# Attention and gated feed-forward on one core: block 0 divided by its sums behind the value products, two maxima taken from PSUM, one group's turn by DVE and DMA, and a new order

## The chip, the cores and the metric

The kernel runs on 1 core of one Trainium2 chip. The metric is the device time of one execution in microseconds; the median of the runs shown is given, and beside it the profiled execution.

## The reference

Inputs are q, k and v of 4 batches, 8 heads, 768 positions and 64 dimensions in float32, and two weight matrices, w_in (512 x 2048) and w_out (2048 x 512).

```
k_sum = k.reshape(B, H, 24, 32, D).max(axis=3)      # one summary key per 32 keys
v_sum = v.reshape(B, H, 24, 32, D).mean(axis=3)
scores = [q.k / 8 where |i - j| < 16 else -1e9,  q.k_sum / 8 + log(32)]
a = exp(scores - max);  a = a / (sum(a) + 1e-9)
x = a @ [v, v_sum]                                   # 3072 tokens x 512
h = x @ w_in;  out = (h * cos(h)) @ w_out
```

## The kernel before

**Blocks and groups.** The 3072 tokens are eight blocks of 384, two to a batch. A block's attention is done in four groups, one for each pair of heads, named a, b, c and d; a0 is pair a of block 0, c1 pair c of block 1. A group has six tiles of 64 queries, and each tile sees 96 neighbouring keys and 24 summary keys, so its scores are 128 x 720 (128 partitions: two halves of 64 queries; 6 times 120 columns).

**One group's path (class Group).** `load_q`, `load_k`, `load_v` (three DMAs) and `load_vs` (two) bring the data. In blocks 0 and 1, PE turns q and k (`turn_q`, `turn_k`) and ACT or DVE copy them out; two products with an identity lay the masks in two PSUM banks (`place_masks`), and `scores` adds the products, one bank for each head. `scale` copies each bank to SBUF (two copies), `maximum` is a DVE reduction over the 720 columns (L588), `less_max` subtracts it on POOL (L593), `exp` runs on ACT (L606), `sums` adds up on DVE (L609, over 121 columns a row, the last a constant 1e-9), `inverse` is a reciprocal on DVE (L614), and `normalize` multiplies on POOL (L617). Then the probabilities are turned: in groups that are not "moved" PE does six transposes (`turn_p`, L626) and ACT or DVE two copies (`place_p`, tile pt); in "moved" groups DVE transposes 32 x 32 squares (`square_p`, L640), one DMA writes them to memory (`move_out`) and four read them back in place (`move_in`). `values` (L670) multiplies v by pt, 12 products, and its output already has the dimensions on the partitions, as the feed-forward needs it. `x_high` rounds it to the matmul format, `x_low` is the rest (DVE, L356, tile xl).

**Feed-forward (class Step).** Step s of a block and a slice f of 128 hidden columns: `up` is 12 products (L714), then ACT and DVE compute the gate (`turns`, `residue`, `sine`, `square`, `gate`), the result is split in a high and a low part, and `down` and `down_low` are nine products (L770). Six steps of block 0 (s0 to s5) come first, then the 16 of block 1, then the other ten of block 0, then the other blocks.

**Weights (class Slice).** A slice f of w_in and w_out, w0 to w15, is loaded by two DMAs of 512 KB and split into a high and a low part of 1024 columns: `magnitude` on ACT (L388), `clamp` (L393), `shift` (L399), `last_bits` (L407) and `first_bits` (L415) on DVE, `high_part` (a cast, ACT or DVE), `low_part` (a subtraction on POOL or DVE). Step s0 needs w0, and so on.

**Order.** The whole order is written out by hand in the string `ORDER`. A token is owner, method and arguments: `a0.tp.0.3` is `turn_p` of the first four tiles of a0 into bank 3, `w5.fb.1` is `first_bits` of slice 5 into stage buffer 1. The loop at the end calls the method of each token in turn, and each engine, and SP for the DMAs, keeps its instructions in that order; waits between engines are put in by the framework.

The short names: q, k, v, m are the loads; tq, tk turns; cq, ck copies; ks key summaries; ms masks; sc scores; z copies of the scores; mx maximum; su less_max; ex exp; sm sums; iv inverse; nm normalize; tp, cp turn and copy of the probabilities; pt, po, pi squares, move out, move in; va values; xh, xl high and low part of x; for slices l, ab, cl, sh, lb, fb, hi, lo in the order of the list above; for steps up, tu, re, si, sq, ga, hi, lo, dh, dl, and ta, tb, st, sb for the results.

## Time and profile before

| | |
|---|---|
| runs shown, median (3 runs) | 663.17 us (660.64 to 663.44) |
| profiled execution | 661.89 us |
| its span, first to last instruction | 660.1 us |
| PE busy | 632.6 us (96%) |
| DVE / ACT / POOL busy | 449.7 / 363.9 / 221.8 us |
| mean granted TensorE clock | 0.987 |

In a row of the timeline the columns are start (us from the span's start), duration, engine, line, operation, output<-input, shapes and count; in brackets stands how long the engine was idle before it and what it waited for. A row of the stretches gives the stretch, its length, and for each engine the busy time and the number of instructions, then the granted clock (1 is 2.4 GHz, 0.5 is 1.2 GHz), the share of the DMA engines and the rate. A row of the chain is start, duration and what held the end of the program at that time. "late", "x" and "sc" are tiles: late buffers hold raw weights and, early on, data of the groups.

### The profile page before, as it was taken

To read this page: it belongs to the slowest core of one execution; us is meant where nothing else is said; L and a number is where in the kernel's file an instruction comes from. 1 tells how busy PE (TensorE), PEld (TensorE's weight loads), DVE (VectorE), ACT (ScalarE), POOL (GpSimd) and SP (SyncE) were. 2 spreads that over 40 slices of the span, in tenths; PEclk is the share of its full clock that TensorE was granted. 3 is DMA by queue.
4 is the path that set the end of the run, shared out by engine and by line. 5 is a ranking of instruction groups with operands and counts; after the bars stand their busy time and mean duration, and the time that the engine had idled before them with its cause. 6 is when DMAs were issued, how large, how long until landed. Compare 5 with 4: busy or idle time off the path is not lost.

```text
span 660.1 us, 13282 instructions
## 1 busy us (share of the span) xinstructions
PE 632.6 (96%) x5141; PEld 560.2 (85%) x5141; DVE 449.7 (68%) x798; ACT 363.9 (55%) x640; POOL 221.8 (34%) x219
## 2 busy tenths in 40 slices
PE   6478999999999999999999999999999999999996
PEld 5256889989988998898898899889889989899985
DVE  4887999887855576668797777576876756433344
ACT  2656977776554485437477464356554645444342
POOL 4784896764430342301323411112330212010110
PEclk9869999999999999999999999999999999999999
DMA  9997906544243244525445433424364332000001
GB/s 224 259 271 203 276 15 223 169 109 71 55 122 85 91 124 132 127 59 114 111 107 135 147 98 97 114 43 85 115 163 104 92 94 70 5 1 17 16 17 48
DMA packets 167158, 72.68 MB, mean 110 GB/s; under 512 B 136824, under 2 KB 155832, under 8 KB 167096
## 3 DMA queue, kind: packets, MB, share of 16 engines
q1 hardware_dynamic: 167096, 71.84, 40.9%
q8 instruction: 40, 0.66, 0.4%
q14 instruction: 22, 0.18, 0.1%
HBM read 53.72 MB, written 15.73 MB: 105 GB/s over the span
## 4 chain that ended last, share of the span: by engine, by line
PE 86%; DMA 5%; SPq 3%; POOL 2%; DVE 1%; issue 1%; ACT 1%; DVEq 0%; POOLq 0%; ACTq 0%
PE banks L770 39%; PE banks L714 39%; PE banks L569 4%; PE banks L670 3%; DMA late<-in_moe_w_out_dram 3%; DMA late<-in_v_dram 1%; SPq L456 1%; POOL w L356 1%; DMA late<-in_q_dram 1%; POOL gl L356 1%; SPq L493 1%; POOL stage L393 0%; ACT stage L388 0%; PE banks L556 0%; DVE m L588 0%
## 5 line engine op out<-in xcount | busy, mean ns | idle before, releaser
L714 PE MATMUL banks<-xh,w 128*128 128x384 f32 x1024 | 272.1, 337 | 0.1
L770 PE MATMUL banks<-w,gh 128*128 128x512 f32 x768 | 198.1, 393 | 0.2 <-ACT gh L350 0.2
L714 PEld LDWEIGHTS banks<-xh,w 128*128 128x128 f32 x1024 | 185.9, 188 | 2.8 <-ACT pt L350 0.4
L714 PE MATMUL banks<-xl,w 128*128 128x384 f32 x512 | 171.4, 335 | 0.0
L770 PEld LDWEIGHTS banks<-w,gh 128*128 128x128 f32 x768 | 142.6, 188 | 29.0 <-ACT gh L350 0.5
L724 ACT ACTIVATE t<-banks 128x384 int32<-128x384 f32 x128 | 62.5, 489 | 133.6 <-DVE gl L356 54.9
L356 POOL TENSOR_TENSOR gl<-t,gh 128x384 fp32r<-128x384 f32 x55 | 56.6, 1029 | 221.4 <-ACT gh L350 86.0
L770 PE MATMUL banks<-w,gl 128*128 128x512 f32 x384 | 109.8, 394 | 0.1
L727 DVE SCALAR_TENSOR_TENSOR t<-t,banks 128x384 f32<-128x384 int32 x128 | 70.0, 548 | 56.9 <-ACT t L724 56.2
L732 ACT ACTIVATE t<-t 128x384 f32<-128x384 f32 x128 | 66.7, 523 | 66.3 <-DVE t L727 66.0
L714 PEld LDWEIGHTS banks<-xl,w 128*128 128x128 f32 x512 | 96.1, 188 | 1.6
L739 DVE SCALAR_TENSOR_TENSOR t<-t,banks 128x384 f32<-128x384 f32 x128 | 69.3, 546 | 41.2 <-ACT t L735 41.0
L770 PEld LDWEIGHTS banks<-w,gl 128*128 128x128 f32 x384 | 71.1, 188 | 14.6 <-DVE gl L356 0.2
L593 POOL TENSOR_TENSOR sc<-sc,m 128x720 f32<-128x720 f32 x28 | 40.1, 1431 | 129.2 <-DVE m L588 129.2
L735 ACT ACTIVATE t<-t 128x384 f32<-128x384 f32 x128 | 65.8, 521 | 2.1
L617 POOL TENSOR_TENSOR sc<-sc,r 128x720 f32<-128x720 f32 x28 | 39.5, 1411 | 51.4 <-DVE r L614 50.3
L350 ACT CAST gh<-t 128x384 fp32r<-128x384 f32 x68 | 34.7, 510 | 33.2 <-PE banks L770 16.5
L356 DVE TENSOR_TENSOR gl<-t,gh 128x384 fp32r<-128x384 f32 x73 | 41.7, 572 | 12.6 <-ACT gh L350 6.5
L356 POOL TENSOR_TENSOR w<-stage,w 128x1024 fp32r<-128x1024 f32 x15 | 36.2, 2416 | 10.0 <-ACT w L350 8.6
L352 DVE CAST gh<-t 128x384 fp32r<-128x384 f32 x60 | 23.2, 386 | 22.2 <-PE banks L770 20.4
L580 DVE SCALAR_TENSOR_TENSOR sc<-banks,mask 128x360 f32<-128x360 f32 x48 | 24.4, 524 | 19.2 <-PE banks L569 19.0
L569 PEld LDWEIGHTS banks<-kd,qd 64*64 64x64 f32 x1344 | 28.4, 135 | 9.4 <-issue 6.7
(102 smaller groups left out, 620.7 us busy)
## 6 DMA issues: line engine op xcount, KB each, us to landing
pd<-stage SPq DMA_DIRECT2D x22, 384.0 KB
late<-in_moe_w_in_dram SPq DMA_DIRECT2D x16, 512.0 KB
late<-in_moe_w_out_dram SPq DMA_DIRECT2D x16, 512.0 KB
pt<-pd SPq DMA_DIRECT2D x66, 96.0 KB
vn<-in_v_dram SPq DMA_DIRECT2D x52, 120.0 KB
out_dram<-stage SPq DMA_DIRECT2D x23, 256.0 KB
kn<-in_v_dram SPq DMA_DIRECT2D x24, 192.0 KB
qn<-in_q_dram SPq DMA_DIRECT2D x92, 48.0 KB
```

The costliest lines, as they stand in the source:

```text
L350: eng.copy(out=out, in_=in_)
L356: eng.tensor_tensor(out=lo, in0=src, in1=hi.bitcast(F32), op=ALU.subtract)
L569: nc.tensor.matmul(out=self.sp[hh][s * QT : (s + 1) * QT, c, lo : lo + n], lhsT=self.qd[rows, t * QT : (t + 1) * QT], rhs=self.kd[rows, ke ...
L593: nc.gpsimd.tensor_tensor(out=self.sc, in0=self.sc, in1=self.m.unsqueeze(2).broadcast_to([P, U, NK]), op=ALU.subtract)
L617: nc.gpsimd.tensor_tensor(out=self.sc, in0=self.sc, in1=self.r.unsqueeze(2).broadcast_to([P, U, NK]), op=ALU.mult)
L714: nc.tensor.matmul(out=self.h, lhsT=w_of(name, self.f)[:, c * P : (c + 1) * P], rhs=x_of(self.blk, part, c), start=n == 0, stop=n == last,)
L724: nc.scalar.activation(out=self.t.bitcast(I32), in_=self.h, func=AF.Copy, scale=1.0 / TWO_PI)
L727: nc.vector.scalar_tensor_tensor(out=self.t, in0=self.t.bitcast(I32), scalar=-TWO_PI, in1=self.h, op0=ALU.mult, op1=ALU.add)
L732: nc.scalar.activation(out=self.t, in_=self.t, func=AF.Sin, scale=0.5)
L735: nc.scalar.activation(out=self.t, in_=self.t, func=AF.Square, scale=math.sqrt(2.0))
L739: nc.vector.scalar_tensor_tensor(out=self.t, in0=self.t, scalar=-1.0, in1=self.h, op0=ALU.add, op1=ALU.mult)
L770: nc.tensor.matmul(out=self.acc[i], lhsT=g[:, i * P : (i + 1) * P], rhs=w_of(name, self.f), start=self.first and n == 0, stop=self.last an ...
```

## The change

Four things:

- `LATE`: in block 0's four groups `sums` and `normalize` go. The probabilities are turned undivided, with the constant column of 1e-9 as a row 121. `values` takes pt as the stationary side and v as the moving one, so its output has the queries on the partitions, and after each of the 12 products a second one with a column of ones gives the sum of its row. `inverse` then reads these sums from PSUM, the new `divide` (xn) multiplies on DVE from PSUM into one SBUF tile shared by the four groups, and the new `turn_x` (tx) turns the result with three transposes on PE; `x_high` and `x_low` follow as before.
- `PMAX`: in a1 and c1, `maximum` reads the scores in PSUM, from two banks side by side, instead of the copy in SBUF.
- `TURNS`: b2 becomes a "moved" group (its six transposes and two copies go).
- A new `ORDER`: 2245 tokens for 2246.

```diff
+PMAX = "00001010000000000000000000000000"
+LATE = "11110000000000000000000000000000"
-TURNS = ("00000000011111111111111111111111", "00000000001111111111111111111111")
+TURNS = ("00000000011111111111111111111111", "00000000011111111111111111111111")
...
+            self.late = LATE[blk * NG + pr : blk * NG + pr + 1] == "1"
+            self.rows = NK + 1 if self.late else NK
+            self.pmax = int(PMAX[blk * NG + pr : blk * NG + pr + 1] or "0")
...
         def maximum(self):
             m = self.m = att.tile([P, U], F32, name="m", bufs=2)
+            if self.pmax:
+                i = self.first_bank
+                nc.vector.tensor_reduce(
+                    out=m.rearrange("p (c h) -> p h c", h=2),
+                    in_=banks[:, i : i + 2, : QC * NK].rearrange("p h (c n) -> p h c n", n=NK),
+                    axis=AX.X, op=ALU.max,
+                )
...
+                return
...
         def inverse(self):
-            if self.fused:
+            if self.late:
+                self.r = att.tile([P, U], F32, name="r", bufs=2)
+                nc.vector.reciprocal(out=self.r, in_=self.xw[:, :, D])
+                return
...
-                nc.tensor.transpose(out=pT[:, t - lo, :], in_=self.sc[:, t, :], identity=ident)
+                nc.tensor.transpose(out=pT[:, t - lo, :], in_=self.all[:, t, : self.rows], identity=ident)
...
         def values(self, i):
+            if self.late:
+                self.xw = bank(i)[:, : U * (D + 1)].rearrange("p (u n) -> p u n", u=U)
+                for t in range(U):
+                    c, s = divmod(t, 2)
+                    for hh in range(2):
+                        p, to = self.pt[2 * c + hh][s], self.xw[s * QT : (s + 1) * QT, 2 * c + hh]
+                        nc.tensor.matmul(
+                            out=to[:, :D], lhsT=p[:NK], rhs=self.vn[:, t, hh * D : (hh + 1) * D],
+                            start=True, stop=True,
+                        )
+                        nc.tensor.matmul(out=to[:, D:], lhsT=p, rhs=ones[: self.rows], start=True, stop=True)
+                return
...
+        def divide(self):
+            nc.vector.tensor_tensor(
+                out=self.xq.rearrange("p (u n) -> p u n", u=U), in0=self.xw[:, :, :D],
+                in1=self.r.unsqueeze(2).broadcast_to([P, U, D]), op=ALU.mult,
+            )
+
+        def turn_x(self, i):
+            self.xps = bank(i)[:, :TB]
+            for c in range(QC):
+                cols = slice(c * P, (c + 1) * P)
+                nc.tensor.transpose(out=self.xps[:, cols], in_=self.xq[:, cols], identity=ident)
...
+    Group.xq = carve(x1[3], 0, P, TB)
```

The new order, by queue, where it matters early. SP before and after (loads):

```
before  ... d0.q w0.l c0.v c0.m w2.l a0.v a0.m d0.m w5.l c1.m b1.q w3.l d1.m c1.q a1.q d0.v w4.l a1.m a1.v b0.m b1.m d1.q b0.v c1.v v1_0.l w8.l
after   ... d0.q w0.l d0.m a0.v w2.l c0.m a0.m w5.l c1.m b1.q c0.v a1.q w3.l d0.v b0.m w4.l c1.q b1.m b0.v a1.v c1.v a1.m d1.q v1_0.l w8.l
```

DVE from v0_0's halving to b0.xl, before and after:

```
before  v0_0.h a0.iv v0_1.s c0.mx w1.cl w1.sh w1.lb w1.fb d0.mx w0.cl c0.sm w0.sh c0.iv w0.lb w2.cl w0.fb d0.sm w2.sh d0.iv w2.lb w2.fb w5.cl a0.xl w5.sh b0.mx w5.lb w5.fb b0.sm c0.xl b0.iv w3.sh a1.mx w3.lb d0.xl w4.cl w4.sh c1.mx w4.lb a1.sm b0.xl
after   v0_1.h v0_0.h v0_1.s c0.mx w1.cl w1.sh w1.lb w1.fb w0.cl d0.mx w0.sh w0.lb w0.fb w2.cl w2.sh b0.mx w2.lb a0.iv w2.fb a0.xn w5.cl c0.iv w5.sh c0.xn w5.lb a0.xl w3.cl w5.fb w3.sh d0.iv c0.xl d0.xn a1.mx w4.cl w3.lb w4.sh c1.mx a1.sm b0.iv d0.xl a1.iv b0.xn w4.lb b0.xl
```

ACT around the same time, before and after:

```
before  w1.ab b0.z.1 b0.z.0 d0.cq d0.ck.1 c0.ex d0.z.1 d0.z.0 w0.ab w1.hi w2.ab a0.cp.0 d0.ex a0.cp.1 w0.hi w5.ab a0.xh c0.cp.0 c0.cp.1 w2.hi
after   w1.ab d0.cq a0.cp.0 b0.z.0 a0.cp.1 d0.z.1 w0.ab d0.z.0 w1.hi w2.ab c0.ex w0.hi b0.z.1 w5.ab d0.ex c0.cp.0 c0.cp.1 w2.hi b1.cq a0.xh
```

PE from a0's value products to s1.up, after:

```
a0.va c0.tp.0 b1.tq c0.tp.1 c0.va a0.tx d0.tp a1.tq a1.ms c0.tx a1.sc d0.va b0.tp.0 c1.tq c1.ms d0.tx b0.tp.1 c1.sc b0.va b1.ms b1.sc b0.tx d1.tq a1.tp.0 s0.up d1.ms a1.tp.1 d1.sc s1.up
```

a1's tokens are `a1.z.1 ... a1.z.0 a1.mx` and c1's `c1.z.1 ... c1.mx c1.z.0`. On PE, between b2.pt and b2.va stand s19.dl, s20.dh, s20.dl, c2.sc, a2.va, s21.dh, s21.dl, s24.up, s25.up and d2.sc. On ACT d1.ex and b1.ex now stand one behind the other. v0_1's halving and the clamp of w3 move from POOL to DVE. The end is now `s127.tb.2.a s127.ta.1.0.v s127.ta.0.1.a s127.sb.2 s127.ta.2.v s127.st.1 s127.st.0 s127.st.2`, where before ACT took the first half of chunk 2 and DVE all the rest.

## Rows read from the trace of the kernel before

**Rows 1.** The page, part 1: busy time, share of the span, instructions.
```profile
PE 632.6 (96%) x5141; PEld 560.2 (85%) x5141; DVE 449.7 (68%) x798; ACT 363.9 (55%) x640; POOL 221.8 (34%) x219
```

**Rows 2.** Busy time by stretch: PE, PEld, DVE, ACT, POOL, clock, DMA share, GB/s.
```profile
21.73:58.88 37.15, 23.28 (x343) 17.02 (x344) 32.32 (x40) 24.11 (x41) 27.04 (x18) 0.77 0.80 216
26.00:42.00 16.00, 7.67 (x69) 6.19 (x69) 15.64 (x20) 9.88 (x15) 11.28 (x7) 0.57 0.92 258
58.88:70.00 11.12, 10.29 (x120) 8.51 (x119) 9.58 (x13) 9.00 (x17) 6.31 (x5) 1.00 1.03 325
70.00:93.00 23.00, 22.73 (x175) 19.46 (x174) 21.46 (x34) 21.03 (x35) 21.56 (x18) 1.00 0.49 137
93.00:655.00 562.00, 562.00 (x4320) 504.98 (x4320) 373.50 (x691) 302.91 (x538) 156.30 (x143) 1.00 0.35 92
```

**Rows 3.** Timeline of PE: a0.va, b1.tq, c0.va, b0.va, start of s0.up.
```profile
32.58 1.65 PE L670 MATMUL banks<-pt,vn 120*64 120x64 f32 x24 [5.44 <-ACT pt L350]
...
37.75 0.88 PE L502 MATMUL banks<-ident,late 128*128 128x128 f32 x3 [2.35 <-DMA late<-in_q_dram]
...
39.26 1.55 PE L670 MATMUL banks<-pt,x 120*64 120x64 f32 x24 [0.21 <-ACT pt L350]
...
56.71 0.92 PE L670 MATMUL banks<-pt,vn 120*64 120x64 f32 x24 [2.27 <-DMA vn<-in_v_dram]
...
58.88 0.43 PE L714 MATMUL banks<-xh,w 128*128 128x384 f32 x1
```

**Rows 4.** Timeline of DVE: v0_0.h, c0.mx, w1.cl, w2.sh, d0.iv, b0.xl, tail copy.
```profile
18.38 1.22 DVE L259 TENSOR_TENSOR late<-late 96x1024 f32<-96x1024 f32 x1 [1.36 <-DMA late<-in_v_dram]
...
21.73 0.89 DVE L588 TENSOR_REDUCE m<-late 128x6 f32<-128x720 f32 x1
22.93 0.70 DVE L393 TENSOR_SCALAR stage<-stage 128x1024 f32<-128x1024 f32 x1 [0.31 <-ACT stage L388]
...
34.87 1.21 DVE L399 TENSOR_SCALAR banks<-stage 128x1024 int32<-128x1024 int32 x1
36.00 0.17 DVE L614 RECIPROCAL r<-r 128x6 f32<-128x6 f32 x1
...
58.18 0.56 DVE L356 TENSOR_TENSOR xl<-banks,xh 128x384 fp32r<-128x384 f32 x1 [1.14 <-ACT xh L350]
...
655.57 0.42 DVE L808 TENSOR_SCALAR last<-banks 128x256 f32<-128x256 f32 x1 [0.63 <-ACT last L806]
```

**Rows 5.** Chain that ended last, early pieces: start, duration, what.
```profile
18.30 7.46 DMA late<-in_moe_w_out_dram
...
25.78 0.33 SPq L477
...
31.82 5.28 DMA late<-in_moe_w_out_dram
```

**Rows 6.** Groups by line and shape, 100 to 655 us: sums, normalize, square_p.
```profile
L617 POOL TENSOR_TENSOR sc<-sc,r 128x720 f32<-128x720 f32 x24 | 33.9, 1414 | 51.4 <-DVE r L614 50.3 <-ACT sc L606 1.0
...
L609 DVE TENSOR_REDUCE r<-sc 128x6 f32<-128x726 f32 x24 | 21.6, 898 | 6.4 <-ACT sc L606 6.2
...
L640 DVE STREAM_TRANSPOSE stage<-sc 128x768 f32<-128x768 f32 x22 | 21.3, 970 | 8.0 <-POOL sc L617 7.9
```

**Rows 7.** Chain that ended last, later pieces: scores, value products, six transposes.
```profile
165.37 1.02 PE banks L569 x36
166.38 0.85 PE banks L670 x24
...
174.34 0.66 PE banks L626 x6
```

**Rows 8.** Timeline of SP's queue: c0.v's first two issues, b1.q.
```profile
19.20 1.99 SPq L477 DMA_DIRECT2D x<-in_v_dram  x2
...
34.11 1.03 SPq L456 DMA_DIRECT2D late<-in_q_dram  x2
```

**Rows 9.** Timeline of ACT: a copy of c1's scores.
```profile
52.58 0.45 ACT L350 COPY late<-banks 128x360 f32<-128x360 f32 x1
```

More of the change, by code (lines that the diff above doesn't have):

```diff
@@ L173 @@
-s123.hi.a s124.si s123.lo.p s124.sq s124.ga s126.up.3 s124.hi.v s124.lo.v s127.up.4 s126.tu s125.tu s125.re s126.re
-s123.dh s126.si s125.si s123.dl s125.sq s126.sq s124.dh s125.ga s125.hi.v s125.lo.v s124.dl s127.tu s125.dh s127.re
-s126.ga s127.si s126.hi.v s127.sq s125.dl s126.lo.v s126.dh s127.ga s127.hi.a s126.dl s127.lo.p s127.dh s127.dl
-s127.ta.2.a s127.ta.0.0.v s127.st.2 s127.tb.2.v s127.st.0 s127.ta.1.1.v s127.sb.2 s127.st.1
+b0.k a0.q a0.k c0.k d0.k b0.tk.0.0 c0.q b0.tk.1.1 a0.tq.2 v0_1.l a0.tk.0.3 a0.tk.1.4 a0.ck.0.a a0.ks.0 v0_0.l
@@ new lines @@
+a0.ms.5.6 a0.ck.1.a a0.ks.1 a0.cq.v c0.tk.0.7 b0.ck.0.v a0.sc b0.q b0.ks.1 c0.ck.0.v c0.tk.1.3 a0.z.1.a b0.ks.0 w1.l
+a0.z.0.v c0.tq.4 a0.mx d0.tk.0.2 c0.cq.a d0.tk.1.6 d0.q c0.ms.0.5 c0.ck.1.a a0.su d0.ks.1 d0.ks.0 c0.ks.0 a0.ex w0.l
+c0.ks.1 v0_1.h.v c0.sc v0_0.h.v c0.z.0.a b0.tq.4 d0.ck.0.a b0.ms.7.3 b0.cq.a v0_1.s.v v0_0.s.p d0.ck.1.a a0.tp.0.0
+c0.z.1.a b0.ck.1.a b0.sc w1.ab.0 c0.mx d0.m d0.tq.2 w1.cl.v c0.su d0.ms.6.1 a0.v d0.cq.a w1.sh.4.5 a0.cp.0.a a0.tp.1.2
+b0.z.0.a d0.sc w2.l a0.cp.1.a w1.lb d0.z.1.a c0.m w0.ab.0 w1.fb.1 a0.m d0.z.0.a w0.cl.v w1.hi.a d0.mx w5.l w1.lo.p
@@ L177 @@
+s123.dl s125.sq s126.re s125.ga s126.si s124.dh s125.hi.a s126.sq s125.lo.p s124.dl s126.ga s125.dh s127.tu s126.hi.a
+s127.re s126.lo.v s127.si s125.dl s127.sq s126.dh s127.ga s127.hi.v s126.dl s127.lo.p s127.dh s127.dl s127.tb.2.a
+s127.ta.1.0.v s127.ta.0.1.a s127.sb.2 s127.ta.2.v s127.st.1 s127.st.0 s127.st.2
 """
@@ L307, in tile_kernel @@
     qd0 = const.tile([P, TB], F32, name="qd")
+    ones = const.tile([P, 1], F32, name="ones")
+    nc.vector.memset(ones, 1.0)
     kmax = const.tile([P, NB // 2, BLOCK // 2], F32, name="kmax")
@@ L551, in score_banks @@
             self.sp = [bank(i)[:, : QC * NK].rearrange("p (c n) -> p c n", c=QC) for i in two]
+            self.first_bank = two[0]
         def place_masks(self, *two):
@@ L597, in exp @@
         def exp(self):
-            self.r = att.tile([P, U], F32, name="r", bufs=2)
-            if self.fused:
+            if not self.late:
+                self.r = att.tile([P, U], F32, name="r", bufs=2)
+            if self.pmax == 2:
+                for u in range(U):
+                    c, h = divmod(u, 2)
+                    nc.scalar.activation(
+                        out=self.sc[:, u, :], in_=self.sp[h][:, c, :], func=AF.Exp, bias=self.m[:, u : u + 1],
+                        accum_out=self.r[:, u : u + 1],
+                    )
+            elif self.fused:
                 for u in range(U):
@@ L623, in turn_p @@
             lo, hi = ((0, 4), (4, U))[j]
-            pT = self.pT[j] = bank(i)[:NK, : (hi - lo) * P].rearrange("p (t n) -> p t n", t=hi - lo)
+            pT = self.pT[j] = bank(i)[: self.rows, : (hi - lo) * P].rearrange("p (t n) -> p t n", t=hi - lo)
             for t in range(lo, hi):
-                nc.tensor.transpose(out=pT[:, t - lo, :], in_=self.sc[:, t, :], identity=ident)
+                nc.tensor.transpose(out=pT[:, t - lo, :], in_=self.all[:, t, : self.rows], identity=ident)
         def place_p(self, j, eng):
@@ L631, in place_p @@
                 self.pts = att.tile([P, U * P], F32, name="pt")
-            pt = self.pts[:NK].rearrange("p (t n) -> p t n", t=U)
+            pt = self.pts[: self.rows].rearrange("p (t n) -> p t n", t=U)
             copy(eng, pt[:, lo:hi, :], self.pT[j])
@@ L846, in tile_kernel @@
     n_v, n_k, n_s = U * P, KC * P, U * NKP
-    x1 = [xp.tile([P, 2 * TB], F32, name=f"x1_{i}", tag=t) for i, t in enumerate(("xh01", "xl01", "xh11"))]
+    x1 = [xp.tile([P, 2 * TB], F32, name=f"x1_{i}", tag=t) for i, t in enumerate(("xh01", "xl01", "xh11", "xl11"))]
     qd1 = carve(late[2], 2 * n_k, P, TB)
@@ L907, in tile_kernel @@
             su="less_max", ex="exp", sm="sums", iv="inverse", nm="normalize", tp="turn_p", cp="place_p",
-            va="values", xh="x_high", xl="x_low",
+            va="values", xn="divide", tx="turn_x", xh="x_high", xl="x_low",
         ),
```

291 lines of the change are left out of this document (145 added, 146 removed).

## The prediction

> **What bounds the kernel now.** The page's first part comes first: PE is busy for 632.6 of 660.1 us [rows 1], so 27.5 us are all the idle time that a new order could give back, and everything else is PE's own work. The table of stretches says where that idle time lies: from 93 to 655 us there is none, from 70 to 93 us 0.27 us, from 58.88 to 70 us 0.83 us [rows 2]; the rest, 26.4 us, lies before 58.88 us and in the last 5 us. PE's timeline gives the moments and what it waited for: a0's value products begin at 32.58 us after 5.44 us for ACT's copy of the turned probabilities (pt), b1's q at 37.75 after 2.35 us for its load, c0's value products at 39.26, b0's at 56.71 after 2.27 us for v, and the first up-projection, s0.up, at 58.88 [rows 3]. From there PE has work in its queue nearly without a gap. So the time of the kernel is **the start of s0.up, plus PE's work behind it, plus what PE idles behind it**, and I price the change in these three.
>
> What sets the start of s0.up is DVE. Between 21.73 and 58.88 us it is busy for 32.32 of 37.15 us, and from 26 to 42 us for 15.64 of 16 [rows 2]; its last low part (b0.xl) starts at 58.18 and runs 0.56 us, and s0.up follows [rows 3, 4]. Its second string is SP's queue: in the chain the issue at 25.78 follows the landing at 25.76 of a transfer issued at 18.30, eight issues earlier, so SP can be held by what has not landed [rows 5].
>
> **Block 0 divided late.** Out go, for each of four groups, the sum over the probabilities (0.90 us on DVE) and the scaling by POOL (1.41) [rows 6]; three of the four sums lie behind 21.73 us, which frees 2.7 us of DVE. In come a division of 128x384 out of PSUM, which I take as the low part of the same shape and source, 0.56 [rows 4]: 2.2 us of DVE. The reciprocal stays (0.17 each), but reads what PE has made. POOL's 5.6 us are worth nothing by themselves: POOL is not the bound before 58.88 us, and from 70 us the four scalings are long done.
>
> PE gets twelve more products a group with one moving column, and three transposes. The twelve are 24 records. Bounds from rows: the 48 records of the scores, of which the chain lists 36, take 1.02 us (0.021 each), the 24 of the values 0.85 (0.035) [rows 7]; 0.5 to 0.85 us, and I take 0.7. A transpose is 0.11 (six in 0.66) [rows 7]. That is 1.0 us a group, 4 us in all, up to twice that while the granted clock is at half (mean 0.57 from 26 to 42 us [rows 2], between the levels of 1.2 and 2.4 GHz). All of it stands ahead of s0.up in PE's queue, where PE has some 21 us of idle time to cover it, so as PE work it costs nothing; only the piece on c0's path counts, and it is in the walk below. The Trainium skill, "TensorE: Matmul & The Clock Gate", section "Wait — 56ns, not 53.3ns?", states that the spacing of small matmuls never falls below about 25 ns, and that about 62 ns each bind where the decode is not done in hardware; by the latter the 24 records would cost, as an estimate from that page, 1.5 us a group, s0.up would come about 0.8 us later, and the sum would be -1.9 instead of -2.7 us. The 0.021 us of the scores' records speak against it, and I keep 0.7.
>
> **A new kind of wait.** Before, the reciprocal followed DVE's own sum. Now a0.iv, c0.iv, d0.iv and b0.iv wait for PE's value products, which wait for ACT's copies and for v; behind each stand the bit passes of the weights, the division and the low parts, and for those wait w5's, w3's and w4's casts and s0.up. I follow DVE's new queue from the latest of the early ones. c0.v is issued behind b1.q rather than at 19.20 us [rows 8]. SP loses some 2.5 us to the wait for v's sums (d0.m now follows the weights directly) and saves as much by c0.v's absence, so b1.q keeps its place, its issue ending near 35.1 us; PE used it 2.6 us after that end [rows 3, 8]. So c0.v is issued until about 37 us and lands near 39.5. c0's value products then begin at 39.5, against 39.26 before, and last 1.55 [rows 3] plus some 0.8 for the new ones at half clock: c0.iv at 41.9. **From there to b0.xl DVE's queue holds** seven passes over a slice (1.21 each), two clamps (0.70), seven divisions or low parts (0.56), three reductions over 720 (0.89) and three reciprocals (0.17), 17.0 us; neighbours overlap by about 0.08 (34.87 + 1.21 against 36.00) [rows 4], so 22 of them take 15.3. That gives 57.2; for b0's round trip through PE and ACT I add 0.2. **s0.up at 57.4, or -1.5 us.** The bounds are from DVE never waiting (54.3, the first rival) to waits like the two longest above (64, the second).
>
> **The maximum taken in PSUM** (a1, c1): worth 0. The idea would save a copy of 0.45 us [rows 9] ahead of each maximum. But DVE's copy at 655.57 waited 0.63 us for ACT, which read the other half of the same bank [rows 4]: reads of one bank by two engines are put in a row. In the new order both copies of a1 stand ahead of a1.mx, which therefore waits for both as before; c1.mx goes ahead of one copy, and that copy then waits for c1.mx, with the subtraction behind it. The bounds are -0.9 (both copies hidden) and +0.9 us (ACT held by c1.z.0 for a reduction), on engines that are not PE; I keep 0.
>
> **b2's probabilities by DVE and DMA.** Six transposes go from PE in the stretch where it never idles: 0.66 us [rows 7]. DVE's transposition costs 0.97 [rows 6] against a copy of 512 columns that goes, and ACT loses a copy of 256: both have room (373.5 and 302.9 of 562 us [rows 2]). SP gets five issues more behind b2.nm. From square to value products the new order leaves PE two up-projections, two and a half down steps, two scores and a value product, some 12 us, which cover a write and a read back; if that cover fell short PE would wait up to 5 us (as the longest pt wait [rows 3]), and I give that no part of the forecast. Gain **-0.66**.
>
> **The rest of the order.** a1's first four transposes move ahead of s0.up: **-0.44** at 0.11 each. v0_1's halving and w3's clamp come from POOL to DVE: 1.22 us, hidden in the 1.36 that DVE waits for v there [rows 4], and 0.70, counted in the walk. d1.ex and b1.ex stand together on ACT, so a pair of table loads goes where ACT has 2 us of room in 23 [rows 2]: 0 on PE. For idle time behind s0.up I keep the 1.1 us of before (0.83 and 0.27); bounds 0 and 4. In the tail the last bank is emptied by ACT and DVE in another split: **-0.1**, bounds ±0.4.
>
> Sum: -1.5 - 0.66 - 0.44 - 0.1 = **-2.7 us**. It is made against the profiled execution, 661.89 us (span 660.1 and 1.8 around it); the median of the runs shown, 663.17, is 1.3 above that, and I keep that distance: **660.5 us**. About 0.5%, 3.3 us, is what a measurement of this kernel can tell from no change, so the forecast itself stands inside.
>
> **Rivals.** *DVE never waits.* Its work between 21.73 us and b0.xl is 32.32 - 2.7 + 2.2 + 0.7 = 32.5 us; without idle time s0.up begins at 54.3, the gain is 4.6 + 1.2 = 5.8, the time 657.4. For it: b0.v now stands ahead of a1.v, a1.m and d1.q in SP's queue, so the 2.27 us wait goes, and the first value products stand free of the reductions. Against: each of the four reciprocals now depends on PE.
>
> *DVE stops at the reciprocals.* Place: a0.iv and c0.iv, in front of w2's and w5's bit passes. If c0's value products slip as a0's did (5.44 us) and b0's as they did before (2.27) [rows 3], DVE stands 7.7 us more, s0.up comes at 65, and the time is 668. It decides from 6 us of such waits on, when c0's products begin after 45.5 us. For it: w2's and w5's absolute values stand ahead of c0.ex and c0's copies on ACT, and wait for transfers like those that took 7.46 and 5.28 us to land [rows 5]; w2 is issued some 2 us later than before. Against: w5, behind which c0's copies stand, is not.
>
> *The late division shortens nothing.* The weights' passes set s0.up at 58.9 with or without it, and new small waits eat the transposes taken from PE: 663.
>
> **How the numbers follow.** The forecast's case has 0.50, between 658.5 and 663, and 0.15 of that is below 659.9; DVE never waiting 0.22; DVE stopped at the reciprocals 0.12; nothing gained 0.16. Faster by over 0.5%: 0.15 + 0.22 + 0.01 = 0.38. Slower: 0.12. Within: 0.50. The range, 656.0 to 665.5, reaches from below the first rival past the third by the 2 us that a run can lie off, and leaves out most of the second. The likeliest case's own range is 658.5 to 663.
>
> **What would show it.** In the profile after: the first up-projection at 57.4 ± 1.5; DVE's wait at c0's reciprocal under 2 us; the 24 records with one column in 0.7 us at full clock; c1's copy held by its maximum; PE idle by about 26 us in all and its busy time 630 to 634; no gap at b2's value products. If s0.up begins before 55.5 or after 60.5, or PE idles by more than 3 us behind it, the forecast is wrong, and the first term or the third names the step.

## The result, and the profile after

The changed kernel takes 665.72 us (median of 19 runs) against 662.67 for the kernel before in the same runs: ratio 1.0048, 95% interval 1.0037 to 1.0058. The ratio is that of the means, without one run of the kernel before that took 788.06 us. The change is half a per cent slower, where 660.5 was forecast, and 0.2 us above the range. The profiled execution took 664.68 us with a span of 662.9; of before it was 661.89 and 660.1. The 2.8 us between the spans are what the two traces can account for.

First the page's first part, of the kernel after (engine, busy us, share, instructions):

```profile
PE 638.4 (96%) x5243; PEld 568.3 (86%) x5243; DVE 444.1 (67%) x791; ACT 370.3 (56%) x645; POOL 210.9 (32%) x221
```

PE has 5.8 us more work than before [rows 1], and DVE and POOL have less, as they should. Next the busy time in two stretches, from a0's value products to s0.up and from there to the last product's end, of the kernel before and then of the kernel after (columns as in [rows 2]):

```profile
32.58:58.88 26.30, 19.60 (x282) 14.44 (x283) 21.95 (x28) 16.17 (x29) 18.67 (x10) 0.76 0.80 215
58.88:655.12 596.24, 595.13 (x4612) 532.95 (x4610) 404.54 (x736) 332.94 (x587) 184.18 (x165) 1.00 0.37 98
```

```profile
34.13:62.00 27.87, 26.09 (x394) 22.33 (x394) 21.96 (x32) 17.72 (x32) 12.83 (x8) 0.77 0.91 211
62.00:657.42 595.42, 593.76 (x4599) 531.71 (x4599) 399.48 (x728) 338.15 (x590) 183.72 (x171) 1.00 0.39 99
```

These rows give the whole account. s0.up begins at 62.00 instead of 58.88, +3.12: a0's value products begin 1.55 later, PE is busy for 6.49 more between the two moments, and idle for 4.92 less (1.78 instead of 6.70). Behind s0.up PE has 1.37 less to do and idles 0.55 more: -0.82. The tail, from the last product's end to the span's end, is 5.48 instead of 4.98: +0.50 (the spans are given to 0.1 us, so a tail is good to 0.05). Sum +2.80.

What the 6.49 us are is seen in the groups of the kernel after (line, engine, operation, output<-input, shapes, count | busy us, mean ns of one | idle before; PEld is the loading of the stationary operand):

```profile
L709 PE MATMUL banks<-ones,pt 121*64 121x1 f32 x96 | 8.2, 206 | 0.0
L709 PEld LDWEIGHTS banks<-ones,pt 121*64 121x64 f32 x96 | 8.0, 182 | 0.0
...
L580 PEld LDWEIGHTS banks<-kd,qd 64*64 64x64 f32 x1344 | 27.7, 132 | 7.9 <-issue 4.5
...
L731 PE MATMUL banks<-ident,x 128*128 128x128 f32 x12 | 2.5, 323 | 0.0
...
L722 DVE TENSOR_TENSOR x<-banks,r 128x384 f32<-128x384 f32 x4 | 2.2, 539 | 0.0
...
L601 DVE TENSOR_REDUCE m<-banks 128x6 f32<-128x720 f32 x2 | 1.8, 905 | 0.4 <-ACT sc L356 0.4
```

The products with the column of ones are the largest piece (busy times of neighbours overlap; what the ones add is worked out below, 5.2 us). With the 12 transposes (1.9, each from its start to the next start) and a1's first four (0.6) some 7.7 us came in. The rest of the stretch runs some 1.2 us shorter, as more of it ran at full clock (the granted clock is 0.50 from 45.25 to 48.66 us before, and 1.00 from 46.97 on after), such as a1's scores, of the kernel before and then after:

```profile
46.36 1.86 PE L569 MATMUL banks<-kd,qd 64*64 64x96 f32 x48
```

```profile
48.50 1.09 PE L580 MATMUL banks<-kd,qd 64*64 64x96 f32 x48
```

The division is 0.54 as taken, and a maximum over PSUM 0.905, like one over SBUF. PE's timeline of the kernel after (columns as in [rows 3]):

```profile
34.13 0.45 PE L705 MATMUL banks<-vn,pt 120*64 120x64 f32 x2 [6.89 <-DMA vn<-vs]
...
39.16 0.90 PE L512 MATMUL banks<-ident,late 128*128 128x128 f32 x3 [0.64 <-DMA late<-in_q_dram]
...
40.78 0.45 PE L705 MATMUL banks<-x,pt 120*64 120x64 f32 x2 [0.30 <-DMA x<-in_v_dram]
...
49.51 0.33 PE L705 MATMUL banks<-x,pt 120*64 120x64 f32 x2
...
51.37 0.70 PE L659 MATMUL banks<-ident,sc 128*121 128x128 f32 x4
...
55.65 0.33 PE L705 MATMUL banks<-vn,pt 120*64 120x64 f32 x2
...
58.10 1.48 PE L567 MATMUL banks<-mask,ident 128*128 128x360 f32 x4 [0.53 <-ACT late L356]
59.51 1.09 PE L580 MATMUL banks<-kd,late 64*64 64x96 f32 x48
60.52 0.55 PE L731 MATMUL banks<-ident,x 128*128 128x128 f32 x3
...
62.00 0.44 PE L772 MATMUL banks<-xh,w 128*128 128x384 f32 x1
...
83.51 0.84 PE L659 MATMUL banks<-ident,late 128*120 128x128 f32 x6 [1.31 <-DVE t L797]
```

The long waits of [rows 3] are gone, for b1's q since PE comes to it later (39.16 for 37.75), for b0's v since it is loaded ahead of a1.v, a1.m and d1.q. Of the products with the added ones, d0's 48 stand from 49.51 to 51.37, 1.86 us against 0.84 for the 24 of before (48.86 to 49.70), each from the first start to the next start on PE. From b0's first value product to s0.up it is 6.35 us, against 2.17 [rows 3]: b1's masks and scores stand in between on PE, and b0's division and transposes. And DVE, of the kernel after:

```profile
44.07 0.20 DVE L643 RECIPROCAL r<-banks 128x6 f32<-128x6 f32 x1 [3.32 <-PE banks L709]
...
58.28 0.19 DVE L643 RECIPROCAL r<-banks 128x6 f32<-128x6 f32 x1
...
58.91 0.52 DVE L722 TENSOR_TENSOR x<-banks,r 128x384 f32<-128x384 f32 x1
...
61.62 0.56 DVE L362 TENSOR_TENSOR xl<-banks,xh 128x384 fp32r<-128x384 f32 x1 [1.05 <-ACT xh L356]
```

It waits 3.32 us at c0's reciprocal, where under 2 was forecast.

The later start of a0's value products has its own wait. Before, they waited last for ACT's copy (5.44 us [rows 3]); after, for the landing of a0's block sums (6.89 us, vn<-vs). SP issues these 1.68 us later, since c0's block sums now stand ahead of them; its rows, of the kernel before and then after:

```profile
27.89 1.66 SPq L493 DMA_DIRECT2D vn<-vs  x2
```

```profile
29.57 1.60 SPq L503 DMA_DIRECT2D vn<-vs  x2
```

### The profile page after: what moved, and what is told of

Same layout as the page of the kernel before. It is cut to its first block, busy times and chain, and to the rows that moved or that the text cites. A ratio compares the mean times of both kernels' runs of the same rounds, so it can differ in the third digit from the quotient of the medians.

```text
span 662.9 us, 13495 instructions
## 1 busy us (share of the span) xinstructions
PE 638.4 (96%) x5243; PEld 568.3 (86%) x5243; DVE 444.1 (67%) x791; ACT 370.3 (56%) x645; POOL 210.9 (32%) x221
## 4 chain that ended last, share of the span: by engine, by line
PE 87%; DMA 6%; SPq 2%; ACT 1%; POOL 1%; issue 1%; DVE 0%; ACTq 0%; POOLq 0%
PE banks L828 40%; PE banks L772 39%; PE banks L580 4%; PE banks L716 3%; DMA late<-in_moe_w_out_dram 3%; SPq L466 1%; DMA late<-in_v_dram 1%; DMA late<-in_q_dram 1%; DMA x<-in_v_dram 1%; SPq L503 0%; PE banks L659 0%; SPq L258 0%; POOL late L650 0%; POOL sc L614 0%; SPq L377 0%
## 5 line engine op out<-in xcount | busy, mean ns | idle before, releaser
L362 POOL TENSOR_TENSOR gl<-t,gh 128x384 fp32r<-128x384 f32 x60 | 60.9, 1016 | 242.0 <-PE banks L828 76.8
L362 DVE TENSOR_TENSOR gl<-t,gh 128x384 fp32r<-128x384 f32 x68 | 39.4, 579 | 25.7 <-PE banks L828 14.5
L650 POOL TENSOR_TENSOR sc<-sc,r 128x720 f32<-128x720 f32 x26 | 36.6, 1407 | 55.4 <-DVE r L647 46.1
L362 POOL TENSOR_TENSOR w<-stage,w 128x1024 fp32r<-128x1024 f32 x15 | 36.6, 2442 | 16.9 <-ACT w L356 14.3
L358 DVE CAST gh<-t 128x384 fp32r<-128x384 f32 x60 | 23.1, 385 | 18.1 <-PE banks L828 16.5
L580 PEld LDWEIGHTS banks<-kd,qd 64*64 64x64 f32 x1344 | 27.7, 132 | 7.9 <-issue 4.5
```

Of the source, the lines that this page charges most:

```text
L362: eng.tensor_tensor(out=lo, in0=src, in1=hi.bitcast(F32), op=ALU.subtract)
L580: nc.tensor.matmul(out=self.sp[hh][s * QT : (s + 1) * QT, c, lo : lo + n], lhsT=self.qd[rows, t * QT : (t + 1) * QT], rhs=self.kd[rows, ke ...
L650: nc.gpsimd.tensor_tensor(out=self.sc, in0=self.sc, in1=self.r.unsqueeze(2).broadcast_to([P, U, NK]), op=ALU.mult)
```

## The experiments

All in one table first; the columns are read from each trace as above. "Busy" and "idle" are PE's from a0's first value product to the last product's end. The ratio is to the kernel before in the same set of runs.

| run | median, ratio [interval] | a0.va | s0.up | last product's end | busy | idle | tail |
|---|---|---|---|---|---|---|---|
| before | | 32.58 | 58.88 | 655.12 | 614.7 | 7.8 | 4.98 |
| after | 665.72, 1.0048 | 34.13 | 62.00 | 657.42 | 619.9 | 3.4 | 5.48 |
| e1 no ones | 665.63, 1.0049 [1.0034, 1.0064] | 32.42 | 60.71 | 655.68 | 615.0 | 8.3 | 5.42 |
| e2 not late | 674.13, 1.0177 [1.0162, 1.0192] | 33.24 | 72.91 | 667.07 | 615.4 | 18.4 | 5.53 |
| e3 c1.q early | 666.75, 1.0069 [1.0051, 1.0087] | 34.92 | 63.20 | 659.50 | 620.5 | 4.1 | 5.50 |
| e4 sums on DVE | 666.39, 1.0051 [1.0033, 1.0069] | 34.10 | 64.56 | 660.17 | 617.1 | 9.0 | 5.43 |
| e5 e1 + e3 | 667.46, 1.0074 [1.0046, 1.0102] | 31.95 | 62.35 | 657.27 | 615.4 | 9.9 | 5.43 |
| e6 no PSUM maximum | 667.06, 1.0066 [1.0048, 1.0083] | 33.31 | 61.19 | 657.37 | 620.0 | 4.1 | 5.43 |
| e7 SP's order | 666.28, 1.0067 [1.0050, 1.0083] | 28.43 | 62.56 | 658.65 | 620.6 | 9.6 | 5.45 |
| e8 e7 + e6 | 666.32, 1.0055 [1.0035, 1.0076] | 28.99 | 61.49 | 656.53 | 618.6 | 8.9 | 5.47 |
| e9 w3 early | 666.04, 1.0050 [1.0032, 1.0067] | 34.89 | 62.47 | 658.56 | 620.0 | 3.7 | 5.34 |
| e10 e9 + e1 | 664.44, 1.0027 [1.0011, 1.0043] | 34.72 | 60.90 | 656.45 | 614.0 | 7.7 | 5.45 |
| e11 old order, late | 670.41, 1.0111 [1.0093, 1.0129] | 34.20 | 67.88 | 664.04 | 621.5 | 8.4 | 5.06 |
| e12 old order, b2 | 661.78, 0.9990 [0.9976, 1.0003] | 33.62 | 58.59 | 654.73 | 615.1 | 6.0 | 4.97 |
| e13 c0 free of b1's q | 667.21, 1.0064 [1.0050, 1.0079] | 36.63 | 64.32 | 660.46 | 620.0 | 3.9 | 5.44 |
| e14 e13 + e1 | 665.89, 1.0042 [1.0028, 1.0056] | 36.28 | 63.11 | 658.05 | 614.3 | 7.5 | 5.45 |
| e15 e11 + e1 | 670.32, 1.0120 [1.0097, 1.0143] | 34.92 | 64.66 | 662.70 | 618.6 | 9.2 | 5.00 |
| e16 old order, b2, b0.v | 663.16, 1.0009 [0.9997, 1.0020] | 33.54 | 59.34 | 657.35 | 615.7 | 8.1 | 4.95 |
| e17 b0 first | 668.71, 1.0077 [1.0055, 1.0098] | 33.39 | 58.81 | 661.79 | 621.4 | 7.0 | 5.41 |
| e18 e17 + e1 | 666.15, 1.0048 [1.0034, 1.0062] | 34.17 | 57.08 | 657.99 | 614.8 | 9.1 | 5.51 |

### The late division and the order, each alone: e2, e11, e15

e2 undoes the late division in the new order, e11 puts it alone into the old one:

```diff
 e2   -LATE = "11110000..."        +LATE = "00000000..."
      -a0.iv a0.xn a0.tx.3 (c0, d0, b0 too)   +a0.sm a0.iv a0.nm ahead of a0.tp.0 (c0, d0, b0 too)
 e11  the old ORDER, PMAX all 0, b2 turned by PE
      -a0.sm a0.iv a0.nm (c0, d0, b0 too)     +a0.iv a0.xn a0.tx ahead of a0.xh (c0, d0, b0 too)
```

> After the change with the late division alone undone in block 0: sums on DVE, scaling on POOL ahead of the turns, no division, no turning back; the new order, the maxima from PSUM and b2's turn stay (x_low of a0, b0, c0 and d0 moved so that no bank is needed twice). Theory P: PE loses some 7 us of products ahead of s0.up, s0.up at 56 to 58, the time 4 to 6 us below after, under the time of before. Theory D: c1's q still lands at 52, s0.up at 59.5 to 60.5, the time 1.5 to 2.5 below after. Theory R: DVE has three sums more and no reciprocal that waits for PE; s0.up earlier by the 3.3 us that DVE waited at c0's reciprocal, if nothing else holds it.

> The late division alone in the order of the kernel before: the four sums and POOL's scalings out; reciprocal, division and three transposes between each group's value products and its high part; maximum, b2 and loads as before. Theory S: the division lengthens PE's queue and the way from b0's value products (which still wait for b0.v until 56.7) to s0.up, from 2.2 to some 5 us: s0.up at 60.5 to 62.5, the span 662 to 664, so the late division by itself costs what the whole change costs. Rival N (the late division is worth what it frees on DVE, and the new order loses it): s0.up at 57.5 to 59, the span 659 to 660.5.

e2 is 1.8% slower than before and e11 1.1%. In e2 PE waits 8.3, 3.7 and 3.1 us for POOL's scalings, for which this order has no room, and the granted clock is at 0.50 from 34.92 to 55.40 us and again from 58.82 to 65.64, so what PE does there takes up to twice as long. In e11 both theories on record were too low: s0.up at 67.88, 9.0 us later. ACT's timeline of e11 shows how (columns as before):

```profile
49.62 0.48 ACT L356 CAST xh<-banks 128x384 fp32r<-128x384 f32 x1 [4.06 <-PE banks L731]
...
58.20 0.48 ACT L356 CAST xh<-banks 128x384 fp32r<-128x384 f32 x1 [3.49 <-PE banks L731]
```

ACT stands in front of each high part until products, reciprocal, division and transposes are through, and w3's and w4's absolute values behind it on ACT come at 49.99 and 58.96 instead of 42.39 and 50.58. e15 takes the products with ones out of e11:

```diff
-                        nc.tensor.matmul(out=to[:, D:], lhsT=p, rhs=ones[: self.rows], start=True, stop=True)
-                nc.vector.reciprocal(out=self.r, in_=self.xw[:, :, D])
+                nc.vector.reciprocal(out=self.r, in_=mask[:, 0, W : W + U])
```

> The late division alone in the order of the kernel before, as e11 (s0.up 67.9), with the products with the column of ones left out, the reciprocal taken of a constant. If the products make the 9 us: s0.up at 60 to 62. If the round trip value products, reciprocal, division, transposes, high part, low part makes them: s0.up at 64.5 to 66.5, as 5 us of products were never more than 1.6 worth in the new order.

s0.up falls by 3.2 to 64.66, as the second reading had it, the median not at all (the last product ends 1.3 earlier). Part of the 3.2 is lost at once: after waits of 1.50 and 0.83 us on PE the granted clock fell to half just behind s0.up, in this stretch of e15:

```profile
65.00:68.42 3.42, 3.42 (x12) 3.32 (x11) 3.42 (x4) 1.87 (x4) 1.24 (x1) 0.50 0.33 70
```

From s0.up to the last product PE is busy for 597.15 us in e15 and 595.19 in e11, with the same 4609 records. So in the old order the round trip, not the products, is the larger part of what s0.up loses (5.8 of 9.0 us are left without them); and the new order is what makes the late division bearable (1.0048 instead of 1.0111). Neither half is good alone, as placed here.

### PE's work taken away in the new order: e1, e4

e1 has the diff of e15, on the kernel after. e4 brings the sums back to DVE and keeps the late division:

```diff
-                        nc.tensor.matmul(out=to[:, D:], lhsT=p, rhs=ones[: self.rows], start=True, stop=True)
      -a0.iv behind a0.va (c0, d0, b0 too)    +a0.sm a0.iv ahead of a0.tp.0 (c0, d0, b0 too)
```

> The twelve one-column products of each group of block 0 are left out, and the reciprocal takes a constant instead of their sums, so the output is divided by the wrong number; all else is as after the change. Theory P (PE's queue is full from a0's value products on, so what is added there moves s0.up): the value products with the sums took 3.27, 3.26, 1.91 and 1.91 us against 1.65, 1.55, 0.92 and 0.92 before, so s0.up comes up to 5.2 us earlier, at 57 to 59, and the time falls by 3 us or more. Theory D (c1's q, issued behind w4's load and landing at 52.2, holds PE): only what stands behind c1.tq counts, 1.0 us, and PE waits longer in front of c1.tq: s0.up near 61, the time down by 1 us. Theory R (DVE's reciprocals and the late a0.m): no change within 0.5 us.

> The late division is kept, but the sums come from DVE's reduction (ahead of the turns, reciprocal right behind it) and not from one-column products: PE loses the 48 records' worth of each group's second half, DVE gains 0.9 us a group, and no reciprocal waits for PE. Theory P: as with the one-column products left out, s0.up at 57 to 59, but DVE's 3.6 us may take part of it back. Theory D: near 61. Theory R: s0.up earlier by up to 3.3 us, the wait of DVE at c0's reciprocal.

Theory P misses in both. In e1 s0.up comes near 61 as theory D had it (60.71), and the last product ends 1.7 us earlier, as a0's products start 1.7 earlier; the median is the same, as theory R had it. In e4 all three miss. In e1 PE has 4.9 us less to do than in the kernel after and idles 4.9 more. What it idles for is seen in the waits of PE in e1 (what waited, for what: us in total, times, longest):

```profile
PE banks L512 <- DMA late<-in_q_dram: 7.6, 3, 3.1
...
PE banks L659 <- DVE t L796: 1.3, 1, 1.3
PE banks L567 <- ACT late L356: 1.2, 1, 1.2
```

The landings of b1's and c1's q, which hid behind PE's longer queue, are waits again (3.12 and 1.46). In e4 PE has 2.8 us less to do and idles 5.6 more, and s0.up comes 2.6 later still. There PE waits 3.23 us for c1's q, and the granted clock falls to half behind it; PE's row and then the stretch (columns as in [rows 2]):

```profile
52.59 0.90 PE L512 MATMUL banks<-ident,late 128*128 128x128 f32 x3 [3.23 <-DMA late<-in_q_dram]
```

```profile
51.35:58.18 6.83, 5.59 (x49) 4.10 (x53) 4.14 (x5) 3.19 (x6) 3.50 (x2) 0.50 0.51 112
```

c1's q is turned at 52.59 us, nearly as in the kernel after (52.25), and from there to s0.up it is 11.97 us instead of 9.75, with less work. Busy times of runs whose clock rose or fell at different moments are therefore not a measure of work alone.

### One load or one maximum at a time: e3, e6, e7, e8, e9

```diff
 e3   c1.q issued ahead of w3.l
 e6   -PMAX = "00001010..."  +PMAX = "00000000..."; c1.mx behind c1.z.0
 e7   SP: a0.v d0.m a0.m w2.l c0.v c0.m w5.l b1.q c1.m a1.q c1.q w3.l d0.v b0.m w4.l b1.m b0.v a1.v
 e8   e7 and e6
 e9   c0.v ahead of d0.m, w3.l ahead of a1.q
```

> After the change with one edit: c1's q is loaded in front of w3 instead of behind w4. Theory D: c1's q lands near 45, PE does not wait at c1.tq, and s0.up moves by what PE then gains. Theory P: PE waited only 0.18 us at c1.tq, so s0.up moves by 0.2 us at most and the time stays within 0.5 us, or rises where w3, w4 or v of d0 and b0 come later. Theory R: no change.

> After the change with the two maxima taken from the copies in SBUF again (c1's maximum moved behind its second copy). PE waited 0.53 us at b1's masks for ACT's copy of c1, which had waited 0.64 for the maximum. Theory M (the maximum from PSUM puts its 0.9 us between the two copies and holds PE): the wait of 0.53 goes, s0.up 0.5 us earlier, the time down by 0.3 to 0.8 us. Theory N (it is worth nothing): within 0.3 us.

> After the change with another order of the loads alone, on SP: a0's v goes into the 3.2 us in which SP waits for v's sums, a0's sums follow d0's at once instead of third, c0's v comes ahead of w5, c1's q ahead of w3. Theory PD: a0's value products begin near 28 instead of 34.1 us, PE's full queue starts that much earlier and the loads no longer hold it: s0.up at 56 to 58, the time 3 to 5 us below after, below the kernel before. Theory R2: s0.up at 61 to 62 and 665 to 666. If w2 and w5 land later for it and DVE stands, in between.

> The other order of the loads and the maxima from SBUF together. Theory PD with M: 0.5 us below the order of the loads alone. Theory N: the same as it. Theory R2: 665 to 666.

> The kernel after with two loads moved on SP: c0.v stands ahead of d0.m as in the kernel before, and w3.l stands ahead of a1.q, so that w3 is issued near 35 us as before and not at 38.3. Theory S (two strings of nearly the same length lead to s0.up: PE's own queue, lengthened by the value products and the columns of ones, and the weights' string, which w3's later landing lengthens through ACT's and DVE's queues): w3's magnitude on ACT starts near 43 instead of 47.2, the weights' string ends 3 us earlier, but PE's queue still holds s0.up at 60 to 61.5; the span falls by 0.5 to 1.5 us against the kernel after. Rival Q (DVE's and ACT's queues as such are too long in the new order, whatever lands when): s0.up stays at 61 to 62.5, the span at 662 to 664.

None gains, and the table shows why. With the products of ones PE's busy time is 620.0 to 620.6 in e3, e6, e7 and e9, whatever the loads do (618.6 in e8, where a0's products ran at the full clock, 1.96 us for 3.25), and in e3, e6 and e9 the idle time was already down at 4. In e6 b1's masks no longer wait for c1's copy, and PE waits 0.78 and 1.37 elsewhere. In e7 and e8 a0's products start 5 to 6 us sooner, and PE idles that much more behind them (9.6 and 8.9). In e9 w3's absolute value starts at 47.75, not near 43, and waits for no transfer: it stands behind ACT's other work, so w3's landing was no bound, and rival Q's numbers are the ones that came (s0.up 62.47, span 663.9).

### Both at once: e5, e10, e13, e14

```diff
 e5   e1 and e3
 e10  e1 and e9
 e13  c0.v ahead of d0.m; b1.tq behind c0.va on PE; the last copies and stores in the old order
 e14  e13 and e1
```

> Both edits of the first set together: the one-column products left out (the output is divided by a constant) and c1's q loaded in front of w3. Alone, neither gave anything: without the products PE waited 1.46 us for c1's q and 3.12 for b1's, and with c1's q early PE had no wait there but was full from 34.92 us to s0.up at 63.20. Theory PD (two limits of nearly the same length stand side by side, PE's full queue and the loads): both off together, s0.up comes at 57 to 59 and the time falls by 3 us or more below after. Theory R2 (a third thing, DVE's or ACT's queue, sets s0.up at 61 to 62 in each of these): no change, 665 to 666.

> As the run before this one, and the products with the column of ones left out, the reciprocal being taken of a constant (so the values are not divided by their sums). Theory S: both strings are cut, s0.up begins at 57.5 to 59, the span falls to 658 to 660. Rival Q: s0.up stays at 60.5 or later, and the span above 661.

> The kernel after with c0.v issued ahead of d0.m (as before), b1's q turned behind c0's value products on PE instead of ahead of c0's last transposes, and the last copies and stores in the order of the kernel before. Theory F (PE is full from a0's values to s0.up; b1's q is a second bound right behind): only the 0.6 to 1.8 us that PE idles there can come back, s0.up at 60 to 61.3. Rival Q (DVE's and ACT's queues hold it): s0.up at 61.5 to 62.5. The tail from the end of the last product to the end: 5.0 if the order of the last copies makes the 0.5 us, 5.5 if it doesn't.

> As e13, and the products with the column of ones left out, the reciprocal taken of a constant (values not divided by their sums). Theory F: with the second bound moved too, taking the 5 us of products away now pays: s0.up at 57.5 to 59.5, the span 2 to 4 us below that of e13. Rival Q: s0.up at 60 to 61, no more than 1.5 us below e13, as in the runs where b1's q still stood in front.

e10 against e9 is the cleanest pair, same order and same chip; the first stretch (a0's values to s0.up) of e9 and then of e10:

```profile
34.89:62.47 27.58, 25.95 (x394) 22.34 (x394) 21.74 (x31) 17.95 (x32) 13.88 (x9) 0.77 0.88 230
```

```profile
34.72:60.90 26.18, 20.26 (x298) 16.38 (x299) 21.68 (x31) 17.80 (x32) 12.81 (x7) 0.80 0.91 219
```

With the 96 records gone PE is busy for 5.69 us less in this stretch (a part of that is the clock, which reached 1.00 at 45.12 us in e10 and at 47.43 in e9), and the stretch is shorter by 1.40; idle time goes from 1.63 to 5.92. s0.up at 60.90 and the span of 661.9 are rival Q's numbers, not theory S's. e10 is the best kernel of the new order, and still 0.27% slower than before, though it leaves the sums out. In e5 s0.up stays at 62.35 where theory PD had 57 to 59. e14 against e13 is like e10 against e9: s0.up 1.2 us sooner (1.6 there), the span 2.4 shorter (2.0 there), with 5.3 us less work and 4.5 more idle time in front of s0.up. The 2.4 is in theory F's range, but moving b1's q added nothing that e10 did not have, so the theory that b1's q is the one bound right behind PE fails. In both a0's products wait for their block sums until 36.6 and 36.3 (34.9 and 34.7 in e9 and e10, where c0.v is issued as early), and s0.up, at 64.32 and 63.11, is later than any theory had it.

### b0's way first: e17, e18

Tokens that keep their place on their engine are left out here.

```diff
      -b0.va.7 ... c1.mx c1.z.0 a1.sm b1.ms b1.sc b0.iv d0.xl a1.iv b0.xn w4.lb b0.tx.6 b1.z.0 d1.tq.7 b0.xh a1.tp.0 b0.xl s0.up.3
      +b0.va.7 ... d0.xl b0.iv b0.xn c1.mx b0.tx.6 b0.xh c1.z.0 b0.xl s0.up.7 a1.sm b1.ms b1.sc a1.iv w4.lb b1.z.0 d1.tq.6 a1.tp.0
```

> The kernel after with b0's reciprocal, division, transposes, high and low part straight behind b0's value products on their engines, and b1's masks and scores, d1's q, a1's first transposes and a1's sum behind s0.up (s0.up in bank 7, d1 in banks 6 and 3). s0.up comes 3.5 to 4.2 us behind b0's value products instead of 6.35, near 59.5. Theory W (two bounds: PE is full from a0's values on, so what goes behind s0.up has to be done there all the same): the last product ends only 0.3 to 1.2 us sooner, the span is 661.5 to 662.6. Rival B (the way behind b0's values is the whole cost): the span falls by as much as s0.up, to 660 to 660.8.

> As e17, and the products with the column of ones left out, the reciprocal taken of a constant (values not divided by their sums). Theory W: with both bounds cut, s0.up near 58 and the last product 2.5 to 4 us sooner than in the kernel after; the span 658.5 to 660.3. Rival B: no more than 0.5 us below e17. Rival L (loads and the weights' passes bound it at what the runs without ones showed so far): the span stays at 661 to 662.

The stretches of e17, then of e18:

```profile
33.39:58.81 25.42, 22.43 (x336) 19.57 (x336) 21.70 (x30) 17.08 (x27) 12.83 (x7) 0.74 0.96 220
58.81:661.79 602.98, 598.98 (x4661) 534.11 (x4659) 403.32 (x732) 340.61 (x594) 187.01 (x173) 1.00 0.39 98
```

```profile
34.17:57.08 22.91, 16.53 (x240) 13.57 (x240) 20.56 (x29) 16.65 (x27) 11.72 (x7) 0.81 1.01 232
57.08:657.99 600.91, 598.24 (x4661) 534.07 (x4658) 401.54 (x732) 340.47 (x594) 186.77 (x173) 1.00 0.39 99
```

This decides what s0.up is worth. It comes 3.2 us sooner in e17 and 4.9 in e18 than in the kernel after, sooner even than before, and the last product ends 4.4 and 0.6 us later: 59 records of b1, d1 and a1 now stand behind it (the stretch's x4661 takes in three more that were still running at its start), PE is busy there for 5.2 and 4.5 us more, and idles 4.0 and 2.7 us. The rival that b0's way is the whole cost falls. Theory W had the reason (what goes behind s0.up has to be done all the same), but not the sign: it forecast the last product 0.3 to 1.2 us sooner. Against e17, e18 is 2.6 us faster in the median, the most that leaving out the products gave anywhere; against the kernel after it gains nothing.

### The old order, b2 and b0.v: e12, e16

```diff
 e12  -b2.tp.0 b2.tp.1 b2.cp.0 b2.cp.1   +b2.pt.1 b2.po b2.pi; b2.va behind s26.up
 e16  e12 with d2.m behind b2.va; b0.m b0.v ahead of a1.m; b0.xh behind b0.va, b0.xl ahead of a1.sm
```

> The kernel before with b2's probabilities turned by DVE and DMA, and nothing else changed. All theories: s0.up unchanged at 58.9, six transposes fewer on PE behind it, the span 0.5 to 0.8 us shorter (659.3 to 659.7) if the way out and back lands in time; a wait for x or pt at b2's value products, and no gain, if it doesn't.

> The kernel before with b2's probabilities turned by DVE and DMA (with d2's block sums loaded behind b2's value products, whose tile they write), b0.v and b0.m issued ahead of a1.m on SP, and b0's high and low parts ahead of a1's sum on their engines. The wait of 2.3 us for b0.v goes; DVE's sum before b0.xl goes behind it: s0.up at 56.7 to 58, the span 1.5 to 2.7 us below that of the kernel before (657.4 to 658.6), of which 0.66 are the transposes. Rival: something else (w5's or w3's passes) holds s0.up at 58.5 and only the 0.66 is had.

In e12 d2's block sums already lie in the tile that b2's value products read, so b2's part of the output is another; the amount of work is the same. Its span is 0.4 us shorter and its median 0.7, an interval that holds no change. From s0.up to the last product PE is busy for 595.17 us against 595.13 before, although six transposes are gone, so one trace does not resolve a term of 0.66 us in this stretch. Turning b2 by DVE and DMA makes no gap in PE's work. In e16 the s0.up forecast, 56.7 to 58, misses too (59.34). It cures the wait for b0.v (value products at 55.64 instead of 56.71), but d1's q, now issued later, holds PE for 1.49 us right in front of s0.up, and 2.7 us of idle time follow behind it; it equals before. No run here beats the kernel before by more than the measurement can tell.

## Why the prediction was wrong, step by step

**The frame held, its use did not.** Start of s0.up, work behind it, idle time behind it: the terms add up in both traces. s0.up is +3.12 us for a forecast -1.5, what stands behind it -0.82 for -1.10, the tail +0.50 for -0.1. But the forecast bargained with the first term alone. In e17 and e18 it moved by several us without the end coming sooner. What counts is PE's work and idle time from a0's values to the end, 622.5 us before and 623.3 after. That difference alone is not beyond what two traces can differ by: e16, no slower than before, has 623.8.

**The step that failed: "PE has some 21 us of idle time to cover it, so as PE work it costs nothing".** 14.7 of those 21.4 us lie ahead of 32.58, before a0's values exist; all added products come later, where before had 6.70, and the 6.49 us of added work left 1.78 of it. With the work as measured, s0.up at 57.4 was out of reach: 32.58 + 26.09 is 58.67 without any idle time at all. I could have read the 6.70 from a stretch that begins at a0's value products. The forecast's own sign of this, PE busy for 630 to 634 us, did not fit its terms either: 632.6 + 4 - 0.66 is 636, and 638.4 was measured.

**The size.** I took 0.7 us a group for the 24 records with one column. d0 and b0 show 1.0 more than before at the full 2.4 GHz, a0 (34.13 to 37.31) and c0 (40.78 to 44.03) some 1.6 more at 1.2 GHz, 5.2 together, 1.3 a group; e9 and e10 give 5.69, with some of the clock in it. For half clock I had allowed up to twice, so the sum for four groups, transposes included, was 4 to 8 us and held what came; what failed is that I put it at nothing. My row was the wrong one: the scores' records take 0.021 us, the new ones 0.039 or more, like the value products, which were my upper bound (0.035). What sets the two apart is not shown: the scores' stationary operands are 64 x 64 and these 121 x 64, but each record has its own LDWEIGHTS in both (L580 x1344 for the 28 groups that share these tiles, 48 a group; L709 x96). The estimate from the Trainium skill, "TensorE: Matmul & The Clock Gate", section "Wait — 56ns, not 53.3ns?", was 1.5 us a group, from its 62 ns a record; on the mean of the four groups that is nearer than my 0.7, at full clock (1.0) mine is nearer. The trace shows 0.039 us a record at full clock, so those 62 ns did not bind here.

**DVE's walk.** c0's value products began at 40.78 for 39.5 and lasted 3.25 for 2.35 (1.55 + 0.8): the reciprocal at 44.07 instead of 41.9, with DVE idle for 3.32. The 0.8 was too little by my own row, which at half clock makes 1.4 of the 0.7. The start of a0's products I did not price at all: c0.m ahead of a0.m on SP made their block sums the last thing they wait for. From there to b0.xl's end it took 18.1 us for 15.3, and "for b0's round trip through PE and ACT I add 0.2" was the other bad term: 6.35 us behind b0's first value product instead of 2.17, and between 6.05 and 6.36 in every run of this order with the late division except e17 and e18. The second rival (DVE stops at the reciprocals) named the right place, with less than half of its 7.7 us; its sign came true, its condition (c0's products after 45.5 us) did not.

**What was right.** PSUM's maximum is worth nothing: c1's copy was held 0.64 us by it, as said, and e6 finds no difference. ACT's row of the kernel after:

```profile
57.59 0.46 ACT L356 COPY late<-banks 128x360 f32<-128x360 f32 x1 [0.64 <-DVE m L601]
```

b2 makes no gap. The transposes taken from the stretch behind s0.up were forecast at 1.10; 1.37 less work was measured (e12 shows how little a difference of this size can be told from one trace), of which 0.55 is lost to idle time (1.31 at 83.51, where d1's transposes wait for a bank that step 3's gate still reads). The tail, forecast at -0.1 within ±0.4, is not among these: +0.50 lies outside that bound.

**What stays open.** Of the 3.12 us, 1.55 are the later start of a0's values. Its wait is the block sums' landing, and the order of the loads does set this start: in e7 and e8, which issue a0.v and a0.m earlier, it is 28.43 and 28.99. But the size is not settled by one trace: with the same loads ahead of them a0's products started between 31.95 and 34.92 in e1, e3, e5, e6, e17 and e18, and between 32.58 and 34.92 in the runs with the old loads (before, e11, e12, e15, e16). From a0's values to the last product the kernel after takes 0.8 us more than before, e9, e6 and e3 1.1 to 2.0 more; but e16 takes 1.3 more too and is no slower, so only the tail is a cost that every run of the new order repeats. How the 3 us between the medians divide among start, stretch and tail stays open. Why without the products of ones no order here falls below some 7.5 us of idle time is not settled: the waits named are q's landings, c1's copy and b0's division, and each that was moved gave way to another, in e4 and e15 with a fall of the clock behind it. The tail of 5.34 to 5.53 comes with the new order (4.95 to 5.06 in every run of the old one), but not from the last copies: with the old ones put back, e13 and e14 have 5.44 and 5.45. It lies behind the stores: nothing is moved from 658.74 to 660.10 us before and from 661.10 to 662.50 after, some 3.6 and 3.7 us behind the last product, so the half microsecond comes after the last stored byte. What it is, is not known.
